# A gated mix of a state-space convolution and a bilinear GLU: the first TensorE work cut to a quarter of the zero columns, and new slack and ranks in the planner's tables

## The chip, the cores and the metric

The kernel runs on one NeuronCore of a Trainium2 chip. The metric is the device time of one execution in microseconds (us). Of each kernel there are timed runs, without a profile, and one profiled execution, whose trace tells what each engine did. The engines are TensorE (PE, with its weight loads shown apart as PEld), VectorE (DVE), ScalarE (ACT), GpSimd (POOL) and SyncE (SP). DMA transfers are issued here by SP and POOL, a few by ACT.

## The reference

For 2048 positions and 512 channels in float32 the reference mixes two results with a gate of one number per position:

```python
g = sigmoid((x * gate_w).sum(-1, keepdims=True))
a = A_ref(x, ...)      # y = irfft(rfft(u, 4096) * rfft(K, 4096))[:2048] + u * D_skip
b = B_ref(x, ...)      # ((x @ w_gate) * (x @ w_up)) @ w_down, inner width 1792
return g * a + (1 - g) * b
```

In A_ref, K[d, l] = 2 Re sum_n C[d, n] exp(A[d, n] dt[d] l) is a convolution kernel of 2048 taps per channel, from 128 complex states.

## The kernel before

**The GLU.** The inner width 1792 is 14 blocks of 128, in four groups of 3, 3, 4 and 4; the positions are four chunks of 512. For each group and chunk, `hidden` multiplies the tokens `xs` with the gate weights into the PSUM tile `pg` and with the up weights into `pu`; ACT copies `pg` to `h`, DVE multiplies by `pu`. `down` multiplies the product with the down weights into the PSUM tile `y` (two buffers), and `evacuate` has ACT scale it by 1 - g into `acc`. Every operand is split in two parts that the fast matmul format holds (`whi` and `wlo`, `dhi` and `dlo`, `hh` and `hl`), so that a product is three matmuls of 128x512, each with its own weight load. These are 2016 of the program's matmuls. The results of the groups are added up in DRAM by accumulating DMAs from POOL (`out<-acc`).

**The convolution.** It is a 4096-point transform done as small matmuls, all into PSUM tiles named `k` (four buffers): `k<-in,w2s` in the first part of the program transforms u (stored to DRAM as `su_d`); DVE and ACT build tables `x` and `v` for 32 channels at a time, and `k_block` makes the taps from them (`k<-v,x`, 64 matmuls); `k<-kt,w1k_t` is the first step of their transform (stored as `sk_d`). Then, for each quarter of the channels, four times: POOL loads a piece of `su_d` and of `sk_d` into `in` (two buffers), `m_second` transforms it (`k<-in,w2s`, in the last quarter `k<-x,w2s` and `k<-v,w2s`), `m_product` multiplies on DVE, and after every second piece `m_inverse` (`k<-y,w3s`) goes back and SP stores to `y_d`. `m_last` (`k<-in,w_t`, at the very end `k<-x,w_t`) makes the positions. These matmuls are float32, which the chip runs as two passes: two weight loads and two matmuls in the trace for one in the program.

**What sets the order.** Each piece of work is registered by `add` with its engine, an estimated duration, what it reads and writes, and a rank. `Work.plan` (L355) then places the pieces one by one: of those that are ready it takes the one with the earliest start, then the lowest rank, then the lowest number; the instructions are issued to the engines in that order, and each engine's queue runs strictly in it. Four tables of numbers bear on the change:

- `ready` (L279): a piece that reads what a transfer brings may be placed only `SURE` us behind the landing that the planner expects.
- `fetched` (L328): PE's program is brought in blocks of 256 instructions; `FETCH` (5.0 us) and `BEHIND` times the transfers then waiting say how late a block may be. PE's work is not placed ahead of that.
- `EASE` (L227): for a kind of work, named by engine, tiles and duration, an addition to its slack, rank or number.
- `count` and the duration of a piece feed both.

All recorded operations stand under line 124 in the profile, the helper that keeps each engine's order; so they are told apart by the tiles' names.

**The beginning.** `first_loads` (L577) clears a tile `acc` on DVE and has PE multiply it by itself into a scratch bank, before the first real data is there: two float32 matmuls of 512 columns.

Of the kernel before, what the change touches and what calls it, by code (L numbers as in the profile page):

```python
# [18 lines left out]
P = 128  # L19
# [150 lines left out]
class Bus:  # L170
# [25 lines left out]
    def add(self, task, at, us):  # L196
        at = max(at, self.now)
        self.serve(self.queues, self.now, at)
        self.now = at
        self.queues[task.engine == "pool"].append([task, us])  # L200
        self.loads.append((at, sum(x[1] for q in self.queues for x in q)))
        return self.serve([[[*x] for x in q] for q in self.queues], at, 1e9)


class Work:
# [16 lines left out]
    TABLE = 1.3  # L222
    ROOM = {"dve": 0.6, "act": 0.4}
    BEYOND = 60
    BEHIND = 1.05

    EASE = {  # L227
        "act:k/e:0.4": (3, 0, 0),
        "act:k/in:0.32": (0.0, 1, 0),
        "act:pb/x:0.31": (0.0, 0, -60),  # L230
        "act:raw/whi:0.62": (0.0, 0, -60),
        "act:t/rt:0.77": (0.0, 0, -200),
        "dve:ev/y:0.6": (3, 0, 0),
        "dve:k/kt:0.42": (0.0, -1, 0),
        "dve:m/v:1.09": (0.0, 0, -20),
        "pool:ts:0.95": (2, 0, 0),
        "sp:in:0.42": (0.0, 1, 0),
        "sp:ri:0.42": (2, 0, 0),
        "sp:w3s/w2s/v:1.3": (0.0, 1, 0),
    }  # L240
    DMA_RATE = 0.33

    SENT = {"sp": 1.15, "act": 1.15, "pool": 1.98}
    LANDED = {"sp": 1.79, "act": 1.79, "pool": 1.5}
    SURE = 2

    def __init__(self):
        self.tags, self.tasks = {}, []
# [30 lines left out]
    def ready(self, task, d):  # L279

        if d.engine == task.engine == "pe":
            return d.end
        if d.dma and d.start > 20.0 and task.engine in ("pe", "act", "dve"):
            return d.end + self.SURE
        return d.end + self.LAG.get(task.engine, 0.03) + (self.PE_LAG if d.engine == "pe" else 0.0)

    def inputs(self, task):
# [40 lines left out]
    def fetched(self, task, start, past, bus):  # L328
# [8 lines left out]
        while b < n1 + (self.BEYOND if step < 0.05 else 0):  # L337
            asked = self.passed(past, b - self.BLOCK - self.LEAD, n0, start, step)
            at = step * (b - n0) if b <= n1 else task.us + 0.11 * (b - n1)
            if asked < start:  # L340
                late = self.FETCH + self.BEHIND * min(bus.load(asked + 1.2), 5.0)
                start = max(start, asked + late - at)
# [107 lines left out]
def gated_mix_kernel(  # L450
# [16 lines left out]
    pe, dve, act, sp, pool_q = (InOrder(tc, e) for e in (nc.tensor, nc.vector, nc.scalar, nc.sync, nc.gpsimd))  # L467
# [3 lines left out]
    add = work.add  # L471
# [18 lines left out]
    def new(pool, tag, shape, dtype=F32, bufs=1, loose=False):  # L490
        return work.tile(pools[pool], tag, shape, dtype, bufs, loose)

    def bank():
        return new("ps_k", "k", [P, D], bufs=4, loose=True)
# [71 lines left out]
    def load_two(key, tile_of, src, one=True):  # L566

        t = tile_of([P, 2, D])
        for k in range(2):
            raws[key(k)] = (t, k)  # L570
        if one:
            add("sp", 0.42, lambda: sp.dma_start(t.t, src), w=[t], dma=512, rank=-1)
        return t

    ws, wd, xs = {}, {}, {}

    def first_loads():  # L577
        in_y = lambda shape: new("mid", "y", shape, bufs=2)
        in_ev = lambda shape: new("mid", "ev", shape, bufs=2)
        in_in = lambda shape: new("mid", "in", shape, bufs=2)  # L580
        xsrc = lambda kt: xT[P * kt : P * kt + P, :D]
        w0 = raws["w0"] = in_ev([P, 2, D])
        xt = [load_two(lambda k, n=n: ("x", 0, 0, 2 * n + k), in_y, None, False) for n in range(2)]
        wsrc = wts[0][:, : 2 * D].rearrange("p (k d) -> p k d", k=2)
        for kt in range(KT):

            t, k, ks = xt[kt // 2], kt % 2, slice(P * kt, P * kt + P)
            add("sp", 0.42, lambda t=t, k=k, kt=kt: sp.dma_start(t.t[:, k], xsrc(kt)), w=[(t, k)], dma=256, rank=-1)
            e, q = ("sp", sp) if kt else ("act", act)
            add(e, 0.42, lambda q=q, ks=ks: q.dma_start(w0.t[:, :, ks], wsrc[:, :, ks]), w=[(w0, ("k", kt))], dma=128, rank=-1)  # L590
        for f in (1, 2):
            load_two(lambda k, f=f: ("w", f, k), in_ev if f == 1 else in_in, wts[f][:, : 2 * D].rearrange("p (k d) -> p k d", k=2))


        zero = new("glu", "acc", [P, D], bufs=3)
        scratch = bank()
        add("dve", 0.2, lambda: dve.memset(zero.t, 0.0), w=[zero], rank=-1)

        def warm():
            for _ in range(2):  # L600
                pe.matmul(scratch.t, zero.t[:, :P], zero.t, start=True, stop=True)

        add("pe", 3.4, warm, r=[zero], w=[scratch], rank=-1, count=8)

    def weights(fs):
        for f in fs:
# [513 lines left out]
    def v_table(b):  # L1120
        ri, (su, di) = ris[b], sus[b]
        v = vtab["v"]

        def copies():
            for c in range(2):
                act.copy(v.t[:, c, :, 0:4], ri.t[:, c, :, W_B])
                act.copy(v.t[:, c, :, 36::4], ri.t[:, c, :, W_A])

        add("act", 1.46, copies, r=[ri], w=[(v, 2)])
        outer(  # L1130
            v, lambda: ri.t[:, :, :, W_A], lambda: su.t[:, :, W_A], lambda: ri.t[:, :, :, W_B],
            lambda: su.t[:, :, W_B], lambda: di.t[:, :, 0:4], [ri, su, di],
        )

        for to, of, n in (((33, 64, 2), (0, 16, 1), 16), ((34, 64, 4), (33, 49, 2), 8)):
            sq = new("tab", "sq", [P, TB, 16])
            dst = [lambda c=c, to=to: v.t[:, c, :, slice(*to)] for c in range(2)]
            src = [lambda c=c, of=of: v.t[:, c, :, slice(*of)] for c in range(2)]
            pair = lambda sq=sq, n=n: sq.t[:, :, :n]

            def sq_act(dst=dst, src=src, pair=pair):
                act.activation(dst[0](), src[0](), AF.Square)
                act.activation(pair(), src[1](), AF.Square)

            k = 0 if n == 16 else 1
            src_parts = [(v, ("r", 0)), (v, ("i", 0))] if k else [(v, 0), (v, 1), (v, 2)]
            us = 0.69 if n == 16 else 0.63
            add("act", 1.17 if n == 16 else 0.89, sq_act, r=src_parts, w=[(v, ("r", k)), sq])
            add(
                "dve", us,  # L1150
                lambda dst=dst, src=src: dve.scalar_tensor_tensor(
                    dst[1](), src[0](), 2.0, src[1](), op0=ALU.mult, op1=ALU.mult
                ),
                r=src_parts, w=[(v, ("i", k))],
            )
            tt(us, dst[0], dst[0], pair, ALU.subtract, [sq], [(v, ("r", k))])
        return v
# [331 lines left out]


    first_loads()
    prologue()
    for t in range(NR // 4):
# [8 lines left out]
    for b in range(NB):  # L1502
# [4 lines left out]
        v, old = v_table(b), x  # L1507
# [63 lines left out]
```

## Time and profile before

| | |
|---|---|
| timed runs | 584.66, 584.83, 585.61 us; median 584.83 us |
| profiled execution | 589.44 us, of which the span from first to last instruction is 587.5 us |
| PE busy | 576.0 us (98% of the span), 5996 matmuls and as many weight loads |
| DVE, ACT, POOL busy | 511.7, 399.1, 113.3 us (87%, 68%, 19%) |
| DMA | 136.28 MB, mean 232 GB/s |
| mean granted TensorE clock | 0.994 |

PE bounds the kernel: it is the work on 91% of the chain that ended last. A row of the timeline has the start in us, the duration in us (of merged rows from the first start to the last end, or the sum), engine, line, operation, tiles out<-in, and in brackets the time the engine stood idle before and what ended that. "issue" is idle time for which the profile shows no wait. A row of the windows view has the stretch, its length, each engine's busy time with the number of instructions, the granted clock, the DMA engines' share and GB/s. Since matmuls are pipelined and their ends modelled, a group of matmuls is best timed from start to start. Only a few idle spells of PE are in this trace, and the prediction shows them.

### The profile page before, as it was taken

The page shows a single profiled execution, that of the slowest core. Times are in us where ns is not written, and L with a number is a line of the kernel's source. Part 1 is how long each engine was busy: PE and PEld are TensorE (multiplying, and loading weights), DVE is VectorE, ACT ScalarE, POOL GpSimd, SP SyncE. Part 2 cuts the span into 40 slices and gives each one's busy share as a digit, 9 for nine tenths or more (in the row PEclk, how much of TensorE's full clock was granted, in tenths as well). Part 3 has the DMA queues.
Part 4 walks back from the last instruction along what each step waited for, and adds up shares of the span by engine and source line. Part 5 has one row for each costly group of instructions (what it writes and reads, how often), then busy time and mean ns, then how long its engine had stood idle before and what let it go on. Part 6 is the DMA issues. An engine that isn't in the chain of part 4 may idle for free.

```text
span 587.5 us, 14848 instructions
## 1 busy us (share of the span) xinstructions
PE 576.0 (98%) x5996; PEld 435.4 (74%) x5996; DVE 511.7 (87%) x812; ACT 399.1 (68%) x891; POOL 113.3 (19%) x159
## 2 busy tenths in 40 slices
PE   8999999989999999999999999999999999999995
PEld 5777777877887777888767678877778777777774
DVE  5999999977999999999999899996899998346745
ACT  4459978987568779975987585699858553333351
POOL 0003222410201141311122301133221004012011
PEclk9999999998999999999999999999999999999998
DMA  8999959996845798999879958889968259799686
GB/s 282 386 331 351 396 211 362 261 253 161 201 147 88 252 266 190 199 260 285 188 229 241 213 136 299 201 212 195 260 162 246 38 150 280 267 331 239 197 188 125
DMA packets 71687, 136.28 MB, mean 232 GB/s; under 512 B 6852, under 2 KB 35780, under 8 KB 69188
## 3 DMA queue, kind: packets, MB, share of 16 engines
q1 hardware_dynamic: 47668, 87.10, 43.0%
q0 software_dynamic: 23392, 47.98, 39.3%
q8 instruction: 47, 0.77, 0.5%
q10 hardware_dynamic: 560, 0.26, 0.2%
q14 instruction: 20, 0.16, 0.1%
HBM read 80.27 MB, written 55.05 MB: 230 GB/s over the span
## 4 chain that ended last, share of the span: by engine, by line
PE 91%; issue 4%; DMA 2%; POOL 1%; ACT 1%; DVE 1%; DVEq 0%; POOLq 0%; ACTq 0%
PE pg L124 26%; PE pu L124 26%; PE y L124 24%; PE k L124 15%; DMA in<-sk_d 1%; DMA y<-in_xT 1%; DMA sk_d<-ev 1%; POOL out L124 1%; POOL in L124 0%; ACT ev L124 0%; DVE y L124 0%; ACT h L124 0%; ACT xs L124 0%; DVE hl L124 0%; DVE dlo L124 0%
## 5 line engine op out<-in xcount | busy, mean ns | idle before, releaser
L124 PE MATMUL pu<-xs,whi 128*128 128x512 f32 x448 | 140.3, 395 | 0.0
L124 PE MATMUL pg<-xs,whi 128*128 128x512 f32 x448 | 139.4, 392 | 0.5 <-ACT whi L124 0.5
L124 PEld LDWEIGHTS pg<-xs,whi 128*128 128x128 f32 x448 | 84.7, 189 | 19.3 <-ACT whi L124 2.1
L124 PEld LDWEIGHTS pu<-xs,whi 128*128 128x128 f32 x448 | 85.4, 191 | 17.4
L124 PE MATMUL pg<-xs,wlo 128*128 128x512 f32 x224 | 90.6, 405 | 0.1
L124 PE MATMUL y<-dhi,hl 128*128 128x512 f32 x224 | 89.6, 400 | 0.6 <-DVE hl L124 0.6
L124 PE MATMUL pu<-xs,wlo 128*128 128x512 f32 x224 | 90.2, 403 | 0.0
L124 PE MATMUL y<-dlo,hh 128*128 128x512 f32 x224 | 87.4, 390 | 0.0
L124 PE MATMUL y<-dhi,hh 128*128 128x512 f32 x224 | 87.2, 389 | 0.0
L124 POOL DMA_DIRECT2D out<-acc x44 | 38.6, 955 | 167.9 <-ACT acc L124 160.0
L124 ACT COPY ev<-k 128x512 f32<-128x512 f32 x112 | 59.3, 598 | 16.5 <-PE k L124 16.5
L124 ACT CAST hh<-h 128x512 fp32r<-128x512 f32 x56 | 34.8, 622 | 45.8 <-DVE h L124 45.6
L124 DVE TENSOR_TENSOR h<-pu,h 128x512 f32<-128x512 f32 x56 | 38.6, 689 | 30.2 <-PE pu L124 29.7
L124 PEld LDWEIGHTS pu<-xs,wlo 128*128 128x128 f32 x224 | 42.6, 190 | 20.1 <-issue 11.4
L124 ACT ACTIVATE acc<-y,ngate 128x512 f32<-128x512 f32 x62 | 41.7, 685 | 22.7 <-PE y L124 20.5
L124 PEld LDWEIGHTS pg<-xs,wlo 128*128 128x128 f32 x224 | 42.4, 189 | 19.8 <-issue 9.5
L124 ACT COPY h<-pg 128x512 f32<-128x512 f32 x56 | 32.8, 586 | 34.9 <-PE pg L124 33.1
L124 PEld LDWEIGHTS y<-dhi,hl 128*128 128x128 f32 x224 | 42.0, 188 | 19.3 <-issue 7.7
L124 PEld LDWEIGHTS y<-dhi,hh 128*128 128x128 f32 x224 | 42.1, 188 | 9.0
L124 PEld LDWEIGHTS y<-dlo,hh 128*128 128x128 f32 x224 | 42.1, 188 | 7.8
L124 DVE TENSOR_TENSOR hl<-h,hh 128x512 fp32r<-128x512 f32 x56 | 38.4, 685 | 3.2 <-ACT hh L124 3.1
L124 PEld LDWEIGHTS k<-v,x 128*32 128x32 f32 x2048 | 29.4, 110 | 7.6 <-issue 7.2
(130 smaller groups left out, 962.9 us busy)
## 6 DMA issues: line engine op xcount, KB each, us to landing
xs<-xs_d SPq DMA_DIRECT2D x36, 512.0 KB, 6.7
out<-acc POOLq DMA_DIRECT2D x44, 256.0 KB, 6.1
raw<-in_wts SPq DMA_DIRECT2D x33, 256.0 KB, 4.5
xs_d<-xs SPq DMA_DIRECT2D x16, 512.0 KB, 7.6
su_d<-ev POOLq DMA_DIRECT2D x32, 256.0 KB, 7.2
y_d<-ts SPq DMA_DIRECT2D x28, 256.0 KB, 5.8
in<-su_d POOLq DMA_DIRECT2D x12, 512.0 KB, 6.6
sk_d<-ev SPq DMA_DIRECT2D x6, 1024.0 KB, 4.9
```

The lines of the kernel that those rows point to most:

```text
L124: got = getattr(self.engine, name)(*args, **kw)
```

## The change

Two kinds of edit. First, the clearing at the beginning covers 128 of the 512 columns, and PE's first work reads that quarter, repeated by a stride of zero: two matmuls of 512 columns as before and one of 128 behind them. Second, numbers of the planner: `BEHIND` goes from 1.05 to 1.3; `SURE` from 2 us for PE, ACT and DVE alike to 3 for PE and 2 for the others; and of the table `EASE`, five entries are dropped and five are new. The work in the program is otherwise the same; the order is planned anew.

```diff
-    BEHIND = 1.05
+    BEHIND = 1.3
     EASE = {
...
-        "act:k/in:0.32": (0.0, 1, 0),
+        "act:ts/xs:0.62": (0.0, 2, 0),
...
-    SURE = 2
+    SURE = {"pe": 3, "act": 2, "dve": 2}
...
-        if d.dma and d.start > 20.0 and task.engine in ("pe", "act", "dve"):
-            return d.end + self.SURE
+        if d.dma and d.start > 20.0 and task.engine in self.SURE:
+            return d.end + self.SURE[task.engine]
...
-        add("dve", 0.2, lambda: dve.memset(zero.t, 0.0), w=[zero], rank=-1)
+        add("dve", 0.06, lambda: dve.memset(zero.t[:, :P], 0.0), w=[zero], rank=-1)
 
         def warm():
-            for _ in range(2):
-                pe.matmul(scratch.t, zero.t[:, :P], zero.t, start=True, stop=True)
-
-        add("pe", 3.4, warm, r=[zero], w=[scratch], rank=-1, count=8)
+            w = zero.t[:, :P]
+            for n in (4, 4, 1):
+                to = scratch.t[:, : n * P].rearrange("p (n d) -> p n d", d=P)
+                rhs = w.unsqueeze(1).broadcast_to([P, n, P])
+                pe.matmul(to, w, rhs, start=True, stop=True)
+
+        add("pe", 3.85, warm, r=[zero], w=[scratch], rank=-1, count=12)
```

How the change moves instructions on PE is shown at four places. The first is the start of PE's program, as a piece of the difference (`acc` is the cleared tile, `k` the scratch bank):

```order
-L1565 UNCONDITIONAL_BRANCH
+L1568 UNCONDITIONAL_BRANCH
 L124 MATMUL k<-acc 128x512 x2
+L124 MATMUL k<-acc 128x128
 L124 MATMUL pg<-xs,whi 128x512 x2
 L124 MATMUL pg<-xs,wlo 128x512
```

One matmul of 128 columns, four PE instructions, stands between the old first work and the first real product.

The second place is the second block of taps, `k<-v,x`, with what stands ahead of it on PE; before:

```order
L124 MATMUL pg<-xs,whi 128x512 x2
L124 MATMUL pg<-xs,wlo 128x512
L124 MATMUL pg<-xs,whi 128x512 x2
L124 MATMUL k<-v,x 32x64 x64
L124 MATMUL pu<-xs,wlo 128x512
L124 MATMUL pu<-xs,whi 128x512 x2
```

and in the changed kernel:

```order
L124 MATMUL y<-dhi,hl 128x512
L124 MATMUL y<-dlo,hh 128x512
L124 MATMUL y<-dhi,hh 128x512
L124 MATMUL pg<-xs,wlo 128x512
L124 MATMUL pg<-xs,whi 128x512 x2
L124 MATMUL k<-v,x 32x64 x64
L124 MATMUL pg<-xs,wlo 128x512
L124 MATMUL pg<-xs,whi 128x512 x2
```

The block moves to an earlier place: counted from the start of PE's program (a matmul as two instructions, a float32 one as four) it begins with instruction 1480 before and with 1424 now.

The third place is in the second quarter of the channels, the third of its four `k<-in,w2s`. Before it stands 52 matmuls of 128x512 behind the second one, in the middle of GLU products:

```order
L124 MATMUL pg<-xs,wlo 128x512
L124 MATMUL pg<-xs,whi 128x512 x2
L124 MATMUL k<-in,w2s 32x512 x16
L124 MATMUL pu<-xs,wlo 128x512
L124 MATMUL pu<-xs,whi 128x512 x2
```

In the changed kernel 103 such matmuls, a `k<-v,x` block and a `k<-y,w3s` block lie between the second and the third:

```order
L124 MATMUL k<-y,w3s 64x128 x64
L124 MATMUL pg<-xs,wlo 128x512
L124 MATMUL pg<-xs,whi 128x512 x2
L124 MATMUL pu<-xs,wlo 128x512
L124 MATMUL pu<-xs,whi 128x512 x2
L124 MATMUL pu<-xs,wlo 128x512
L124 MATMUL pu<-xs,whi 128x512 x2
L124 MATMUL pu<-xs,wlo 128x512
L124 MATMUL pu<-xs,whi 128x512 x2
L124 MATMUL pu<-xs,wlo 128x512
L124 MATMUL pu<-xs,whi 128x512 x2
L124 MATMUL k<-in,w2s 32x512 x16
```

The loads for it keep their places on POOL: two `out<-ts`, then `in<-su_d`, `in<-sk_d`, the same pair again, then `out<-acc`.

The fourth place is PE's end. Before, the second half of `k<-x,w_t` stands directly ahead of the last two `y` tiles (24 matmuls):

```order
L124 MATMUL y<-dhi,hl 128x512
L124 MATMUL y<-dlo,hh 128x512
L124 MATMUL y<-dhi,hh 128x512
L124 MATMUL k<-x,w_t 32x512 x8
L124 MATMUL y<-dhi,hl 128x512
L124 MATMUL y<-dlo,hh 128x512
L124 MATMUL y<-dhi,hh 128x512
```

Now both halves stand together, 21 `y` matmuls ahead of those 24:

```order
L124 MATMUL y<-dhi,hl 128x512
L124 MATMUL y<-dlo,hh 128x512
L124 MATMUL y<-dhi,hh 128x512
L124 MATMUL k<-x,w_t 32x512 x16
L124 MATMUL y<-dhi,hl 128x512
L124 MATMUL y<-dlo,hh 128x512
L124 MATMUL y<-dhi,hh 128x512
```

Between the matmul that ends the last `y` tile but three and the first matmul of the last `y` tile but one, which needs its buffer, there were three `y` matmuls and half of `k<-x,w_t`; now there are the three `y` matmuls alone.

More of the change, by code (lines that the diff above doesn't have):

```diff
@@ L232 @@
         "act:t/rt:0.77": (0.0, 0, -200),
+        "act:ts/xs:0.62": (0.0, 2, 0),
         "dve:ev/y:0.6": (3, 0, 0),
-        "dve:k/kt:0.42": (0.0, -1, 0),
-        "dve:m/v:1.09": (0.0, 0, -20),
+        "dve:in/whi/wlo:0.69": (0.0, 1, 0),
+        "dve:k/in:0.42": (3, 0, 0),
+        "dve:k/ri:0.7": (0.0, 1, 0),
+        "pe:kt/k/ri/e:2.13": (0.0, 0, -200),
         "pool:ts:0.95": (2, 0, 0),
-        "sp:in:0.42": (0.0, 1, 0),
-        "sp:ri:0.42": (2, 0, 0),
         "sp:w3s/w2s/v:1.3": (0.0, 1, 0),
```

## Prediction

> **What bounds the kernel now.** I read the page first, then the list of waits of PE, then the timeline at each of those waits.
>
> ```profile
> PE 576.0 (98%) x5996; PEld 435.4 (74%) x5996; DVE 511.7 (87%) x812; ACT 399.1 (68%) x891; POOL 113.3 (19%) x159
> q8 instruction: 47, 0.77, 0.5%
> PE 91%; issue 4%; DMA 2%; POOL 1%; ACT 1%; DVE 1%; DVEq 0%; POOLq 0%; ACTq 0%
> ```
>
> PE is busy 98% of the span and is 91% of the chain that ended last. Its matmuls are the same in both kernels but for one small one, so an order can only win what PE idles or runs slowly. All its waits, in total, times and longest:
>
> ```profile
> PE k L124 <- issue: 1.8, 1, 1.8
> PE k L124 <- DVE acc L124: 1.5, 1, 1.5
> PE k L124 <- DMA in<-sk_d: 1.2, 1, 1.2
> PE y L124 <- DVE hl L124: 0.6, 1, 0.6
> PE pg L124 <- ACT whi L124: 0.5, 1, 0.5
> ```
>
> That is 5.6 us, of which 2.0 (1.5 and 0.5) are the beginning. The largest lies in the second block of taps; the rows are the timeline of PE, two stretches of the windows view, and the instruction queue in the DMA view from 129.8 to 130.8 us:
>
> ```profile
> 128.62 1.98 PE L124 MATMUL k<-v,x 128*32 128x64 f32 x125
> 132.36 0.30 PE L124 MATMUL k<-v,x 128*32 128x64 f32 x3 [1.76 <-issue]
> ...
> 130.20:133.65 3.45, 1.69 (x36) 1.25 (x26) 2.70 (x5) 1.84 (x11) 0.55 (x1) 1.00 0.76 150
> 133.65:137.06 3.41, 3.41 (x10) 2.63 (x9) 1.36 (x3) 2.61 (x7) 0.00 (x0) 0.50 0.47 141
> ...
> q8 instruction: 1, 0.02, 5.6%
> ```
>
> 125 of the block's 128 matmuls ran, then PE stood 1.76 us for nothing that waits on a semaphore. The page has 47 packets of 0.77 MB on the instruction queue, 16.4 KB each; 5996 matmuls and 5996 loads over 47 are 255 instructions a packet; and the one packet near lands in this second. So I read the stall as PE's own program coming late. In the stretch of 3.45 us around it PE worked 1.69, and in the next 3.41 the granted clock was 0.50, which costs half, 1.71 us.
>
> The second wait is for a transfer; the last row is the chain of waits:
>
> ```profile
> 317.82 1.60 POOL L124 DMA_DIRECT2D in<-su_d  x1
> 326.36 0.92 POOL L124 DMA_DIRECT2D in<-sk_d  x1 [6.94 <-issue]
> ...
> 331.52 1.15 PE L124 MATMUL k<-in,w2s 32*32 32x512 f32 x32 [1.16 <-DMA in<-sk_d]
> ...
> 326.36 4.91 DMA in<-sk_d
> ```
>
> POOL stood 6.94 us ahead of this load, it was under way 4.91 us, and PE waited the last 1.16.
>
> **The profiled time and the median.** The profiled execution took 589.44 us (span 587.5 and 1.94 around it). Less 1.76, 1.71 and 1.16 that is 584.81, and the timed median is 584.83. The agreement is closer than I may claim, but it says that the timed runs hold little of these three: their transfers are less crowded, or the parts differ and cancel. This decides the forecast, since what isn't lost in a timed run can't be won there.
>
> **The change, part by part.** *The beginning.* Rows of the timeline, then of the windows view:
>
> ```profile
> 0.92 0.48 DVE L124 MEMSET acc<- 128x512 f32 x1 [0.92 <-PEq L1560]
> 1.39 0.17 DVE L124 MEMSET skip<- 128x128 f32 x1
> 1.46 3.78 PE L124 MATMUL k<-acc 128*128 128x512 f32 x4 [1.46 <-DVE acc L124]
> 5.30 0.40 ACT L124 CAST whi<-ev 128x256 fp32r<-128x256 f32 x1
> 5.75 1.22 PE L124 MATMUL pg<-xs,whi 128*128 128x512 f32 x2 [0.51 <-ACT whi L124]
> 9.76 1.05 PE L124 MATMUL pu<-xs,whi 128*128 128x512 f32 x2
> 11.62 0.62 PE L124 MATMUL pu<-xs,whi 128*128 128x512 f32 x2
> ...
> 3.95:7.36 3.41, 2.90 (x6) 1.34 (x5) 1.88 (x4) 2.12 (x5) 0.00 (x0) 1.00 1.10 354
> 7.36:10.77 3.41, 3.41 (x10) 2.64 (x9) 3.24 (x15) 2.18 (x6) 0.00 (x0) 1.00 0.97 335
> ```
>
> A quarter of the columns is cleared in about 0.17 us (the row of `skip`, the same shape) in place of 0.48: PE starts 0.31 us sooner, at 1.15. The added matmul is two passes of a quarter of 3.78/4, 0.47 us. The first work ends at 1.15 + 3.78 + 0.47 = 5.40, where it ended at 5.24. The first real product still waits for ACT's `whi`, which ends at 5.70: on the path this is 0, and PE idles 0.35 us there in place of 0.51.
>
> What it could move is the clock. Two matmuls took 1.05 us at 9.76 and 0.62 at 11.62, so PE ran at half speed until about 10.77, although the clock column says 1.00 there. Laying the 3.41 us of the slow stretch back from 10.77: the stretch to 10.77 was wholly busy and full speed followed; the one to 7.36 was busy 2.90 of 3.41 (85%) and did not bring it. With 0.16 us less idle that is 3.06, 90%. Nothing says that 90% does what 85% didn't, so I take 0.
>
> The Trainium skill ("TensorE: Matmul & The Clock Gate", "What's actually happening") says that the full clock is granted after a busy window of about 3.4 us, and that the windows run free of the kernel's start. The trace agrees with the length (3.41). By that rule the gain depends on how the windows fall in each run, and it is the second rival.
>
> If the clock did rise at the first work, the gain is bounded by DVE, which feeds PE here:
>
> ```profile
> 13.93 0.69 DVE L124 TENSOR_TENSOR h<-pu,h 128x512 f32<-128x512 f32 x1 [1.59 <-PE pu L124]
> 25.15 0.69 DVE L124 TENSOR_TENSOR h<-pu,h 128x512 f32<-128x512 f32 x1 [0.28 <-PE pu L124]
> ```
>
> DVE waited for PE 1.59 and 0.28 us up to the place at 28 us where PE waits for DVE (0.6, `hl`): a faster PE wins at most 1.87 us and then waits longer there.
>
> *The second block of taps* (`BEHIND`). A block of PE's program ends at the same instruction number in both orders. The stall came after 249 or so of the block's 256 instructions, number 1480 + 249 = 1729. In the new order the block has 1424 to 1679, and 1729 falls behind it, among GLU matmuls. What counts is PE's time over the instructions between the asking for a packet and its need. A stretch of the same number of instructions that reaches back over the block holds 249 short and the rest long ones before, 256 short ones now: seven long ones fewer. Long ones take 113 ns, from the row
>
> ```profile
> 16.88 2.72 PE pu L124 x12
> ```
>
> (12 matmuls and 12 loads, 2.72/24). So PE comes there 0.79 us sooner, and `BEHIND`, meant to hold such work back, does not lengthen the lead here. With the profiled transfers the stall would be 1.76 + 0.79 = 2.55. In a timed run without a stall before it is 0 to 0.79; I take 0, since the lighter transfers that hid it leave unknown room. Below nothing is excluded.
>
> The Trainium skill ("Runtime: NRT & Kernel Launch", "Instruction fetch mechanics") holds that fetching is hidden, as dispatch is slower than the refill. By it this place costs 0 in every run and the slower rival falls away. The trace disagrees with 1.76 us in a block that issues 250 instructions in 1.98.
>
> *The third `k<-in,w2s`* (`SURE` 3 for PE). Between the second and third there are 51 more GLU matmuls (51 x 0.227 = 11.6 us) and two `k` blocks of about 2 us each: 15 us more cover, while POOL's order there stays. The wait of 1.16 is gone. What is late next: the fourth piece stands right behind, but its loads follow the third's directly on POOL, so the cover holds for it too. In a timed run that is between 0 and -1.16; by the agreement above I take 0.
>
> *The end.* Rows of the timeline:
>
> ```profile
> 573.75 0.40 PE L124 MATMUL y<-dhi,hh 128*128 128x512 f32 x1
> 574.19 1.37 ACT L124 ACTIVATE acc<-y,ngate 128x512 f32<-128x512 f32 x2 [1.62 <-PE y L124]
> 574.76 1.09 PE L124 MATMUL k<-x,w_t 64*32 64x512 f32 x16
> 575.78 0.50 PE L124 MATMUL y<-dhi,hl 128*128 128x512 f32 x1
> 581.14 0.39 PE L124 MATMUL y<-dhi,hh 128*128 128x512 f32 x1
> 581.57 0.88 DVE L124 SCALAR_TENSOR_TENSOR kt<-y,ngate,kt 128x256 f32<-128x256 f32 x2 [0.28 <-PE y L124]
> ```
>
> The matmul at 573.75 ends a `y` tile; ACT starts on it 0.44 us later and one of its two takes 0.69, so the buffer is free at 574.88. Three `y` matmuls behind leave PE ready at 573.75 + 4 x 0.227 = 574.66; before, half of `k<-x,w_t` (1.02 us to 575.78) covered the rest. Now nothing does: +0.22. One run of `k` less saves one change between shapes; no row shows it alone, 0 to 0.2 from the 0.1 by which `k` rows overlap what follows; -0.1. From 581.14 to the end the same DVE steps and stores follow.
>
> *The other entries of* `EASE` reorder work that lies beside PE. Queue for queue I found no consumer of a transfer on PE that stands clearly closer to its load, so 0; DVE, 87% busy, is their cover, and a table that came late would cost its lateness on PE.
>
> Sum for the timed median: 584.83 + 0 + 0 + 0 + 0.22 - 0.1 = **584.9 us**, no change.
>
> **Rivals.** 0.2%, 1.17 us, is about what a measurement of this kernel can tell from no change.
>
> 1. *The timed runs do hold the transfer wait*, and the agreement was chance. Then 584.83 - 1.16 + 0.12 = 583.8. For: the load is late by POOL's 6.94 us, not by a hair. Against: the sum. Still within 0.2%; only with a little more it is faster.
> 2. *The clock rises during the first work.* Then up to 1.87 is won: 583.1. For: the busy spell at the beginning grows from 3.78 to 4.25 us, 0.84 longer than one stretch instead of 0.37, so if the stretches fall anywhere, in 25% instead of 11% of runs one lies wholly inside. Against: in the other runs nothing moves, and a median of few runs shows mostly those.
> 3. *Slower: PE's program comes late behind the second block* at instruction 1729. The stall is up to 2.55 us, and from the point where it empties about half of a stretch, as 1.69 of 3.45 did, the clock halves for 3.41 us, 1.71 more: up to 584.83 + 2.55 + 1.71 + 0.12 = 589.2; with half the stall and the slow clock 587.9, with the stall alone 586.2 to 587.5. For: the lead is shorter. Against: the timed runs showed nothing of it before.
> 4. *The planner's numbers don't act*: the waits of PE come out as before. Then 584.9 again.
>
> **How the numbers follow.** The forecast with rival 4 0.40, rival 1 0.20, rival 2 0.15, rival 3 0.18, and 0.07 for a new wait elsewhere of a microsecond or two. Faster: 0.15, 0.08 of rival 1 and 0.05 from the edge of the forecast, 0.28. Slower: 0.18 and the 0.07, 0.25. Same: the rest, 0.47. The range runs from rival 2 (583.1, and a little) to rival 3 without the full price: 583.0 to 587.4. The forecast's own range is 583.8 to 585.7.
>
> **What would show it.** In the new profile: PE's first work at about 1.15 and the first product still at 5.75; the clock up near 10.8; no wait of PE for `in<-sk_d` around 330; an "issue" wait or none behind the second `k<-v,x`; a wait of about 0.2 us of `y` for ACT ahead of the last two tiles; from the last matmul to the end 6 us. The forecast is wrong if PE's waits sum to over a microsecond more or less than what the timed runs held, or if the time moves without them.

## The result, and the profile after

The changed kernel is faster. Over 22 runs of each, side by side, it takes 581.98 us (581.00 to 584.79) against 585.56 us (581.94 to 589.93) before: a ratio of 0.9935, with a 95% interval of 0.9917 to 0.9952. The forecast of 584.9 us and its range from 583.0 are missed by 2.9 and 1.0 us. The profiled execution after took 581.93 us, with a span of 580.1.

The page after, its rows of busy time and of the chain's shares by engine:

```profile
PE 573.5 (99%) x5998; PEld 433.8 (75%) x5998; DVE 510.9 (88%) x812; ACT 401.6 (69%) x891; POOL 113.5 (20%) x159
...
PE 97%; DMA 1%; ACT 1%; DVE 1%; issue 0%; DVEq 0%; ACTq 0%
```

The list of PE's waits after (us in total, times, longest):

```profile
PE k L124 <- DVE acc L124: 1.1, 1, 1.1
PE pg L124 <- ACT h L124: 0.7, 1, 0.7
PE y L124 <- DVE hl L124: 0.6, 1, 0.6
PE pg L124 <- ACT whi L124: 0.4, 1, 0.4
```

The waits for "issue" (1.8) and for `in<-sk_d` (1.2) are gone; a new one for ACT's `h` (0.7) has come. The timeline after, at the beginning, the second taps, the third `k<-in,w2s` of the second quarter, the new wait, and the end:

```profile
1.06 4.21 PE L124 MATMUL k<-acc 128*128 128x512 f32 x6 [1.06 <-DVE acc L124]
5.62 1.17 PE L124 MATMUL pg<-xs,whi 128*128 128x512 f32 x2 [0.35 <-ACT whi L124]
6.86 0.62 PE L124 MATMUL pu<-xs,whi 128*128 128x512 f32 x2
...
121.05 1.99 PE L124 MATMUL k<-v,x 128*32 128x64 f32 x128
...
343.43 1.14 PE L124 MATMUL k<-in,w2s 32*32 32x512 f32 x32
...
421.71 0.50 PE L124 MATMUL pg<-xs,wlo 128*128 128x512 f32 x1 [0.67 <-ACT h L124]
...
575.99 0.39 PE L124 MATMUL y<-dhi,hh 128*128 128x512 f32 x1
576.41 0.88 DVE L124 SCALAR_TENSOR_TENSOR kt<-y,ngate,kt 128x256 f32<-128x256 f32 x2 [1.97 <-PE y L124]
577.32 0.36 ACTq L124 DMA_DIRECT2D out<-kt  x1
```

Two matmuls take 0.62 us from 6.86 on, so full speed began at 6.6, where it began at 10.8 before. All 128 matmuls of the taps run through in 1.99 us. The row at 343.43 has no wait. And one thing stands at the end that no part of the prediction has: from PE's last product to the end of the span it is 580.1 - 575.99 = 4.1 us, where it was 587.5 - 581.14 = 6.4 us. So there are four candidates for 3.6 us: the beginning (theory C in the expectations below), PE's late program with the slow clock behind it (theory P), the transfer (theory T), and the end (theory E).

### The profile page after: what moved, and what is told of

The parts are those of the page before. It is cut to its first block, busy times and chain, and to the rows that moved or that the text cites. A ratio compares the mean times of both kernels' runs of the same rounds, so it can differ in the third digit from the quotient of the medians.

```text
span 580.1 us, 14843 instructions
## 1 busy us (share of the span) xinstructions
PE 573.5 (99%) x5998; PEld 433.8 (75%) x5998; DVE 510.9 (88%) x812; ACT 401.6 (69%) x891; POOL 113.5 (20%) x159
## 4 chain that ended last, share of the span: by engine, by line
PE 97%; DMA 1%; ACT 1%; DVE 1%; issue 0%; DVEq 0%; ACTq 0%
PE pg L124 27%; PE y L124 27%; PE pu L124 27%; PE k L124 16%; DMA y<-in_xT 1%; ACT h L124 0%; DVE y L124 0%; ACT acc L124 0%; ACT xs L124 0%; DVE hl L124 0%; DVE dlo L124 0%; DVE kt L124 0%; DVEq L1568 0%; ACT whi L124 0%; DVE h L124 0%
## 5 line engine op out<-in xcount | busy, mean ns | idle before, releaser
L124 PE MATMUL pu<-xs,whi 128*128 128x512 f32 x448 | 138.2, 390 | 0.0
L124 PEld LDWEIGHTS pu<-xs,whi 128*128 128x128 f32 x448 | 84.1, 188 | 17.0
L124 PEld LDWEIGHTS pg<-xs,wlo 128*128 128x128 f32 x224 | 42.1, 188 | 21.5 <-issue 10.1
L124 DVE TENSOR_TENSOR v<-m,v 128x896 f32<-128x896 f32 x32 | 34.0, 1084 | 0.2
```

Of the source, the lines that this page charges most:

```text
L124: got = getattr(self.engine, name)(*args, **kw)
```

## The experiments

Of the kernel before there were between 17 and 30 runs beside each of the four sets of experiments, with medians of 585.60, 585.18, 586.26 and 585.34 us. "Order of before" means that every engine's instructions stand row by row as in the kernel before, but for the edit.

**1. The changed order with the old first work.**

```diff
-        add("dve", 0.06, lambda: dve.memset(zero.t[:, :P], 0.0), w=[zero], rank=-1)
+        add("dve", 0.06, lambda: dve.memset(zero.t, 0.0), w=[zero], rank=-1)
...
-            for n in (4, 4, 1):
...
+            for _ in range(2):
+                pe.matmul(scratch.t, zero.t[:, :P], zero.t, start=True, stop=True)
```

> The changed kernel in its own order, with only PE's first work as it was before (128x512 cleared, two matmuls of 512 columns). The order of everything else is the changed kernel's, row by row; PE's program is 4 instructions shorter at the front. Theory P (the timed runs of the kernel before do hold PE's late program behind the second taps, 1.76 us, and the slow clock after it, 1.71, and the new order loses them): the first work is worth little, 582.0 to 582.5 us, where the changed kernel has 581.98; in the profile full speed is reached near 10.8 us. Theory C (the gain is the clock that rises sooner at the beginning): most of the gain goes, 583.5 to 585.0. Theory T (the gain is the transfer in<-sk_d and the rest of the order): as P, 582.0 to 582.5.

Measured: 582.23 us (7 runs, 581.59 to 583.16), 0.25 more than the changed kernel, which is within the spread of the runs. The beginning isn't where most of the gain comes from. And the clock rose early with the old work too. The windows view of this kernel, with the stretch that ends where full speed began:

```profile
3.11:6.52 3.41, 2.95 (x5) 0.98 (x4) 1.08 (x3) 1.62 (x4) 0.00 (x0) 1.00 1.02 323
```

**2. The order of before with the new first work; 3. with 24 more instructions ahead of it; 4. with both.** Run 2 has the first work of the change. Run 3 keeps the full clearing and cuts the two matmuls of 512 columns into eight of 128, so that each of PE's program packets begins 24 instructions earlier in the work. Run 4 has nine matmuls of 128 columns on the cleared quarter, 28 instructions.

```diff
-            for _ in range(2):
-                pe.matmul(scratch.t, zero.t[:, :P], zero.t, start=True, stop=True)
+            for _ in range(2):
+                for n in range(4):
+                    pe.matmul(scratch.t[:, n * P : n * P + P], zero.t[:, :P], zero.t[:, n * P : n * P + P], start=True, stop=True)
```

That is run 3; run 4, where `w` is the cleared quarter, has this in place of the two:

```diff
+            for n in range(9):
+                pe.matmul(scratch.t[:, n % 4 * P : n % 4 * P + P], w, w, start=True, stop=True)
```

> The kernel before in its own order, with only PE's first work as in the change (a quarter cleared, two matmuls of 512 columns and one of 128, all reading the quarter); the planner's numbers for it are left, so the order is the one before, row by row, and PE's program is 4 instructions longer at the front. Theory P: within 0.5 us of the kernel before (585.56 over 22 runs), so 585.0 to 586.0; the stall behind the second taps may be there or not in its profile. Theory C: 583.3 to 584.3, as DVE's waits allow at most 1.87 us, and full speed from 6.6 us in the profile. Theory T: 585.0 to 586.0.

> The kernel before in its own order and with its own full clearing; only the two first matmuls of 512 columns are cut into eight of 128 over the same columns. This adds 24 instructions at the front of PE's program (32 in place of 8) and so moves every boundary of its packets 24 instructions earlier in the work. At the second taps the asking then falls 24 long instructions sooner (24 x 0.113 = 2.7 us) and the need 24 short ones sooner (0.2 us): 2.5 us more lead than the 11.77 of the profile before. Theory P: the stall of 1.76 and the slow clock of 1.71 go: 585.56 less 1.8 to 3.5 is 582.1 to 583.8, and the runs lie closer together than the 8 us of the kernel before. Theories C and T: 585.2 to 586.0, with the spread unchanged.

> The kernel before in its own order with both: a quarter cleared as in the change, and the first work cut into nine matmuls of 128 columns that read it (36 instructions in place of 8, so the packets' boundaries lie 28 instructions earlier; the first work's columns are those of the change). Nothing of the planner's new order is in it. Theory P alone: 582.1 to 583.8. Theory C alone: 583.3 to 584.3. P and C together: 580.2 to 582.5, so as fast as the change without its order. Theory T: 585.2 to 586.0.

Measured, with 585.60 before: 583.24 us (582.52 to 584.38), 583.51 (582.56 to 584.79) and 582.99 (582.57 to 584.31), 12 runs each. Moving the packets without touching the columns is worth 2.1 us, in timed runs, as theory P has it. But run 2 gave as much, against P's expectation and near theory C's 583.3 to 584.3, and the two do not add up in run 4. Run 2 has 4 more instructions ahead of the work as well, so it could be the boundary there too; and in run 3's profile full speed began at 7.14 us, not near 10.8, so the beginning could have a share there.

**5. Only 4 instructions, without the new first work.** The second matmul of 512 columns is cut into two of 256.

```diff
-            for _ in range(2):
-                pe.matmul(scratch.t, zero.t[:, :P], zero.t, start=True, stop=True)
+            pe.matmul(scratch.t, zero.t[:, :P], zero.t, start=True, stop=True)
+            for n in range(2):
+                pe.matmul(scratch.t[:, 2 * n * P : 2 * n * P + 2 * P], zero.t[:, :P], zero.t[:, 2 * n * P : 2 * n * P + 2 * P], start=True, stop=True)
```

> The kernel before in its own order, with its full clearing; only the second of PE's two first matmuls is cut into two of 256 columns. The columns are the same, PE's program is 4 instructions longer at the front, as with the change's first work, and the first work starts and ends as before. It separates what the run with the change's first work left mixed (583.24 us, against 585.6 before). Theory P (the packet's boundary at the second taps, moved by 4 instructions, gives 0.45 us more lead, and that is enough): 583.0 to 584.2. Theory C' (it is the earlier start and the clearing, not the boundary): 585.2 to 586.0. If the clock at the beginning were late in part of the runs whatever the first work is, both kernels would hold it and the difference here would still be only the boundary's.

Measured: 583.47 us (582.51 to 585.42, 12 runs), against 585.18 before; ratio 0.997 (0.9952 to 0.9989). PE's second taps in its profile:

```profile
128.58 1.99 PE L124 MATMUL k<-v,x 128*32 128x64 f32 x128
```

The stall is gone. Four instructions at the front, with the same work in the same time, are worth 1.7 us (0.6 to 2.8 by the interval), and full speed began late here too, at 10.66 us. With the new first work it is 0.23 less (run 2), which the spread of the runs does not resolve. Theory P holds for the timed runs.

**6. The kernel before, unchanged, profiled once more.**

> The kernel before, unchanged, for a second profile of it. Theory P (the late program at the second k<-v,x belongs to this order, not to one execution): a wait of 1 to 2 us named issue at the second k<-v,x again, with the packet landing 9 to 11 us after the asking. If the profile before caught a rare run: no such wait.

This execution took 586.39 us. Two rows of the list of PE's waits:

```profile
PE k L124 <- issue: 1.9, 1, 1.9
PE k L124 <- DMA in<-sk_d: 1.4, 1, 1.4
```

And PE's timeline at the second taps:

```profile
126.98 1.98 PE L124 MATMUL k<-v,x 128*32 128x64 f32 x125
130.85 0.30 PE L124 MATMUL k<-v,x 128*32 128x64 f32 x3 [1.89 <-issue]
```

Both waits are there again, at the same places. Full speed began at 7.6 us this time, and no slow clock followed the stall. So the stall isn't the mark of one execution. And it is PE's program: counted over all of PE's records, the stall stands ahead of number 1730 in both profiles, and the stalls of over a microsecond in experiments 7 and 10 stand ahead of 1730, 4802 and 6594, which lie whole multiples of 256 apart.

**7. What the packet waits for.** The packet is seen to land in the DMA view. When PE asks for it isn't in the trace; I take the start of PE's instruction 320 ahead of the packet's first one (matmuls and weight loads counted); this is an assumption. For run 5 and for the second profile of before, the DMA view of the microsecond in which it landed:

```profile
q8 instruction: 1, 0.02, 5.9%
```

(run 5, 123.9 to 124.9 us), and the same for before (128.5 to 129.5 us):

```profile
q8 instruction: 1, 0.02, 5.6%
```

| order of before | asked | landed | after us | stall of PE |
|---|---|---|---|---|
| before, first profile | 120.59 | 130.74 | 10.1 | 1.76 |
| before, second profile | 118.96 | 129.49 | 10.5 | 1.89 |
| run 5 (4 earlier) | 120.10 | 124.88 | 4.8 | none |
| run 2 (4 earlier) | 117.92 | 122.38 | 4.5 | none |
| run 3 (24 earlier) | 115.98 | 122.27 | 6.3 | none |

The first row and run 5 have the late clock at the beginning, which puts both some 2 us later. Four instructions sooner are 0.45 us at the 113 ns of a long one, and the packet lands over 5 us sooner. It is the same in all profiles of this order: without the move it took 9.8 to 10.5 us (four profiles: the two of the table, that of the next edit, and that of `BEHIND` alone in experiment 10, whose order is the old one there), with a move of 4 to 28 instructions 4.5 to 6.9 (seven). A constant time to land would not do that. My guess was that the packet is asked for on the other side of something in the queues, and SP's `raw`, issued 1.14 us ahead of the asking in the kernel before, was the suspect.

```diff
-        for t in self.plan():
+        order = self.plan()
+        raw, late = (next(t for t in order if t.engine == "sp" and t.n == n) for n in (513, 499))
+        order.remove(raw)
+        order.insert(order.index(late) + 1, raw)
+        for t in order:
             t.fn()
```

> The kernel before with PE's program, its packets' boundaries and PE's order untouched; on SP's queue the raw load that stands between two and one out stores (at 119.45 us in the profile before) goes out behind the one store instead, some 3 us later, at about 122.8. Theory Q (what decides is on which side of this transfer the packet is asked for): in the profiles of this same order of SP the packet asked for 1.14 and 1.15 us after that raw was issued took 10.14 and 9.82 us to land, and the one asked 0.69, 0.11 or less after it took 4.8, 4.5 and 6.3. Then the packet is now ahead of it and lands some 5 us after the asking, the stall is gone at an unchanged boundary, and the time is as with the boundary moved by 4, 583.0 to 584.0, where the kernel before has 585.2 to 585.6. Theory L (PE's lead alone decides, the transfers don't matter): the stall stays, 585.0 to 586.0. If the later raw makes ACT's cast late (its slack is about 1 to 2 us): a wait of PE a few us behind, and 584 to 586 with the packet early all the same.

Measured: 586.42 us (582.57 to 589.22, 12 runs), against 586.26. SP's timeline in this run, where the moved `raw` goes out with the next one:

```profile
120.74 1.00 SPq L124 DMA_DIRECT2D raw<-in_wts  x2
```

And PE's timeline at the second taps:

```profile
130.13 0.30 PE L124 MATMUL k<-v,x 128*32 128x64 f32 x3 [1.65 <-issue]
```

The `raw` went out 3 us later and the packet still took 10.2 us. Theory Q falls. Whether the packet queued behind something else stays open: that it lands 5 us sooner when four instructions more stand at the front is measured, the reason isn't.

**8. The transfer on another queue.** Run 3, with the third piece's `in<-sk_d` on SP, which stood idle there.

```diff
-                lambda w=w, rows_m=rows_m: pool_q.dma_start(
+                lambda w=w, rows_m=rows_m: (sp if w and (q, T) == (1, 2) else pool_q).dma_start(
```

> The kernel with the packets 24 instructions earlier (583.51 us), with one more thing: the transfer in<-sk_d for the third k<-in,w2s of the second quarter goes out on SP's queue in place of POOL's. In its profile POOL stood 7.11 us ahead of it, while SP stood idle from 313.34 to 326.98. PE waited for this transfer 1.16 us in the profile before, and 0.29, 0.43 and 1.6 in the three since in that order. Theory T (this wait is held in timed runs, and is the rest of the gain that the packets' boundary and the first work don't account for, 583.0 to 582.0): the wait is gone and the time is 582.3 to 583.0. If the rest of the gain is elsewhere in the order: 583.2 to 583.8, with the wait gone all the same. If SP issues it late or it holds up what stands behind it on SP (w2s, pb): slower than 583.5.

Measured: 582.79 us (581.88 to 584.76, 12 runs), 0.72 less than run 3 (582.56 to 584.79). The two overlap widely, and the kernel before was itself 0.42 us lower beside this run, so the pair alone doesn't show a gain. SP's row for the transfer, in the timeline:

```profile
310.03 0.38 SPq L124 DMA_DIRECT2D in<-sk_d  x1
```

And PE's row for the third piece:

```profile
324.34 1.14 PE L124 MATMUL k<-in,w2s 32*32 32x512 f32 x32
```

No wait is left. In the seven profiles with this load on POOL in the order of before the wait was 1.2, 0.4, 0.3, 1.6, 0.3, 0.9 and 1.4 us, 0.9 in the mean, so a gain of that size in timed runs would fit theory T; the next run decides it.

**9. The three together in the order of before** (run 4 with the edit of run 8).

> The order of the kernel before with three edits together: PE's first work as in the change (a quarter cleared), cut into nine matmuls of 128 columns so that the packets lie 28 instructions earlier, and the transfer in<-sk_d for the third k<-in,w2s on SP's queue. Without the last it had 582.99, and the last was worth 0.7 us (583.51 to 582.79). If the causes add up: 582.1 to 582.5, and what is left to the changed kernel's 581.98 is the rest of its order, 0.1 to 0.5 us. If the rest of the order is worth nothing: 581.7 to 582.1. If the first work brings nothing: 582.6 to 583.0.

Measured: 582.02 us (6 runs, 581.89 to 582.71). Three small edits, without any of the planner's new numbers, give the changed kernel's time. Against run 4, which lacks only the transfer's edit, it is 0.97 us less, and the two hardly overlap (run 4 from 582.57 on): theory T holds, with 0.7 to 1.0 us by the two pairs. Against run 8 the new first work is worth 0.77 here.

**10. One part of the planner's numbers alone.** `BEHIND` at 1.3 in the kernel before; and `SURE` by engine in the kernel before.

```diff
-    BEHIND = 1.05
+    BEHIND = 1.3
```

> The kernel before with only BEHIND at 1.3 and the order that the planner then makes. PE's order is the one before, row by row, up to row 656 of 1640, so the second taps, their packet and the lead there are those of before. Theory P: the gain at the second taps is not there; 584.5 to 586.5, by what the order behind row 656 happens to bring, and the profile may show the stall of 1 to 2 us at the second k<-v,x. If BEHIND is what brings the gain: 582.0 to 583.5.

> The kernel before with only the slack behind landings by engine (3 us for PE in place of 2; nothing else differs) and the order that the planner then makes. Its second taps begin at instruction 1423 of PE, as in the change (1424 there with 4 more at the front), so the block lies wholly ahead of the boundary at which the kernel before stalled. Theory P: the stall is gone with this part alone, 582.0 to 584.0. Theory T: the third k<-in,w2s has its cover as in the change, which belongs to the same figure. If the gain is of several parts that only together bring it: 584.5 to 586.

Measured: 595.41 us (592.93 to 598.29) and 597.79 us (595.74 to 599.72), 6 runs each: ratios of 1.0179 and 1.0216. Each part alone is slower by 10 to 13 us, which no theory expected. With `BEHIND`, the largest row of PE's waits:

```profile
PE k L124 <- issue: 3.1, 4, 1.2
```

and two rows of PE's timeline, at the second taps and at the very end:

```profile
129.73 0.30 PE L124 MATMUL k<-v,x 128*32 128x64 f32 x3 [1.21 <-issue]
...
577.47 1.09 PE L124 MATMUL k<-x,w_t 64*32 64x512 f32 x16 [0.47 <-issue]
```

With `SURE`, the largest row of PE's waits:

```profile
PE k L124 <- issue: 4.3, 3, 2.1
```

the row of PE's timeline with the longest of these three:

```profile
263.11 0.69 PE L124 MATMUL k<-y,w3s 32*64 32x128 f32 x3 [2.09 <-issue]
```

and the stretch in the windows view behind it, with the granted clock at 0.50:

```profile
263.08:266.50 3.42, 3.39 (x10) 2.48 (x11) 1.01 (x2) 0.87 (x2) 0.00 (x0) 0.50 0.92 226
```

With `BEHIND` alone PE's order is the old one up to row 656, and the stall at the second taps is there as in the kernel before: theory P again. The rest is new. The program comes late at other places, once with the slow clock behind it. The last of these waits in each, 0.47 and 0.56 us ahead of the second `k<-x,w_t`, are of another kind: they don't stand at a packet's first instruction. And most of the loss is at the end. The planner put the last `k<-x,w_t` behind all `y`, so that ACT, DVE and the stores follow it: with `BEHIND` it is 592.6 - 577.97 = 14.6 us from PE's last matmul to the end, with `SURE` 597.9 - 583.44 = 14.4, where it was 6.4. An order is found for the numbers as a whole; the worth of one number can't be read by setting it alone.

**11. A longer first work in the changed kernel.** The last small matmul has 224 columns in place of 128.

```diff
-            for n in (4, 4, 1):
+            for n, d in ((4, P), (4, P), (2, 112)):
```

> The changed kernel with the last small matmul of PE's first work at 224 columns in place of 128 (96 more, 0.35 us more), the same number of instructions and the same order. PE then works from 1.06 to about 5.6 without the 0.35 us of idle time ahead of the first product, so every stretch of 3.41 us behind the first is wholly busy. In ten profiles so far a stretch with 2.88 to 2.95 us of work brought the clock twice and failed three times, one with 3.06 or more never failed. Theory K (3.06 of 3.41 is already always enough): 581.7 to 582.3, as the changed kernel (581.98), with full speed at 4.5 to 8 us. Theory K' (the idle 0.35 us still costs a late clock in some runs, which are those above 583.4, 5 of 22): the median 581.5 to 581.9 and no run above 583.4. If the first product is held up by the longer first work: up to 0.1 slower.

Measured: 582.16 us (581.52 to 582.59, 6 runs). The changed first work is long enough; six runs are too few to say more of the upper end.

**12. The end.** Run 9 and the changed kernel have the same time, yet PE's last product starts at 573.97 us in the profile of the one and at 575.99 in that of the other. The same 56 pieces of work are the last in both orders. One run puts those of run 9 into the changed kernel's order, the other those of the changed kernel into the old order; `end` is the list of their numbers.

```diff
-        for t in self.plan():
+        order = self.plan()
+        last = {t.n: t for t in order[-len(end):]}
+        for t in order[: -len(end)] + [last[n] for n in end]:
             t.fn()
```

> The order of the kernel before with the three edits (582.02 us), and with the last 56 pieces of work put into the order that the changed kernel has there (the same 56 pieces on both sides; the two halves of k<-x,w_t then run as one, ahead of y, and the last two out<-x go out from POOL some 3 and 8 us earlier before PE's last product). Theory E (the changed kernel's end is worth about 1.9 us by itself: from PE's last product to the end of the span 4.1 us there against 6.1 with the old end; on PE it costs 0.26 for the y tile that waits for ACT and saves about 0.5 for one run of k less): 579.9 to 580.5, faster than both kernels. Theory F (the end is set by the last store in any order, and the shorter end of the changed kernel only mirrors something ahead of it): 581.7 to 582.3, with 6 us behind the last product again.

> The changed kernel with its last 56 pieces of work put into the order that the kernel before has there; nothing else is changed. Theory E: from PE's last product to the end 6.0 us in place of 4.1, 1.9 us more, less the 0.26 of the y tile and plus about 0.5 for one more run of k: 583.6 to 584.4. Then the changed kernel's gain of 3.6 us holds this end too, and its order loses about 2 us to the order before elsewhere on PE (the wait of pg for h, 0.7, among it). Theory F: 581.7 to 582.3.

Measured: 580.59 us (6 runs, 580.14 to 581.52), ratio 0.9908 (0.9873 to 0.9942); and 583.85 us (12 runs, 583.17 to 584.75). The new end is worth 1.4 us on the old order and 1.9 on the new. Theory E holds from both sides, and the first of these kernels beats both the kernel before and the changed one. Rows of POOL, PE and ACT in its timeline:

```profile
566.87 2.89 POOL L124 DMA_DIRECT2D out<-x  x2 [6.97 <-DVE x L124]
...
574.08 0.39 PE L124 MATMUL y<-dhi,hh 128*128 128x512 f32 x1
...
575.41 0.35 ACTq L124 DMA_DIRECT2D out<-kt  x1
```

and SP's queue (`q1`) and POOL's (`q0`) in its DMA view, from ACT's store to the end (packets, MB, share of 16 engines):

```profile
q1 hardware_dynamic: 253, 0.32, 30.2%
...
q0 software_dynamic: 12, 0.00, 1.3%
```

The same rows in the timeline of the changed kernel with the old end:

```profile
573.03 1.28 POOL L124 DMA_DIRECT2D out<-x  x1 [1.43 <-DVE kt L124]
...
575.43 0.39 PE L124 MATMUL y<-dhi,hh 128*128 128x512 f32 x1
...
576.77 0.35 ACTq L124 DMA_DIRECT2D out<-kt  x1
```

and the two queues in its DMA view, from 576.7 us to the end:

```profile
q1 hardware_dynamic: 438, 0.67, 34.4%
q0 software_dynamic: 385, 0.19, 29.1%
```

With the old end, POOL's last accumulating store `out<-x` goes out 2.4 us before PE's last product and is still moving when the last store `out<-kt` goes out; from that store to the end it takes 582.03 - 576.77 = 5.3 us. With the new end POOL's queue is all but empty by then (12 packets) and it takes 578.3 - 575.41 = 2.9 us. SP's four stores `out<-kt` start earlier too, 4.4 us ahead of PE's last product in place of 1.6, and leave 0.32 MB for this stretch in place of 0.67. So that the new order of these pieces shortens the end is shown; how much of it is POOL's stores and how much SP's isn't, since no run moves the one without the other.

## Why the prediction was wrong, step by step

**The step that failed first: "it says that the timed runs hold little of these three".** The profiled time less three losses came to 584.81, next to a median of three runs of 584.83, and I took the agreement as a sign that timed runs don't pay the losses. Two things were wrong with it. Three runs say little about a kernel whose runs spread over 8 us: the median of 22 is 585.56. And the profiled execution held a fourth loss which I left in, the late clock at the beginning. Runs 2 and 5 differ in the first work alone; in their profiles full speed began at 5.03 and at 10.66 us, and PE's last product started at 574.49 and 576.67, with the same waits between, about 2.2 us apart:

```profile
574.49 0.39 PE L124 MATMUL y<-dhi,hh 128*128 128x512 f32 x1
...
576.67 0.39 PE L124 MATMUL y<-dhi,hh 128*128 128x512 f32 x1
```

Less that too, the profiled time is 584.81 - 2.2 = 582.6, and 582.79 is what the order of before takes with the stall and the transfer wait gone (run 8). So timed runs do hold them, some 2 us for the program (1.7 in run 5, 2.1 in run 3) and 0.7 to 1.0 for the transfer. By the second profile the same subtraction gives 586.39 - 1.89 - 1.40 = 583.1, and the median lies 2.5 us above that.

The slow clock behind the stall, the 1.71 of that subtraction, is in a part of the timed runs. Each run's record has its mean granted clock: it is 0.994 or 0.995 in 19 of the 87 runs of the kernel before beside the experiments, as in its first profile (0.994), and these have a median of 587.2 us against 585.2 for the others. In none of the 66 runs of experiments 2 to 5, 8 and 9, which have no stall there in their profiles, is it below 0.996. A stretch of 3.41 us at half clock takes 0.003 off the mean of such a run, so I read the 19 as runs with the slow clock; where it stood in them isn't recorded.

**The second taps.** That the block's new place shortens the lead was right: counted as in experiment 7, it is 9.4 us from asking to need (119.15 to 128.55) against 11.77 with the stall of 1.76, so 10.0 without it: 0.6 less, where 0.79 was said. That the stall would therefore be 0 to 0.79 us, or 2.55, was wrong, because the time to land isn't a constant: 5.3 us there after the change, 10.1 to 10.5 before. I also put the move down to `BEHIND`; with `BEHIND` alone the block keeps its place (run 10), and with `SURE` alone it moves. Rival 3 (slower) fell with it.

The Trainium skill ("Runtime: NRT & Kernel Launch", "Instruction fetch mechanics") has fetching hidden behind dispatch. By it run 5, four instructions and no other work, would have been worth nothing; it was worth 1.7 us, and the measurement decides.

**The third `k<-in,w2s`.** The cover was right and the wait is gone; taken as 0, it was worth 0.7 to 1.0 us. That is rival 1, whose 583.8 was too high only because the rest wasn't in it.

**The beginning.** PE starts at 1.06 (1.15 was said) and the first product at 5.62 (5.75 was said), so that start itself wins 0.13 us at most: right in the main. "Nothing says that 90% does what 85% didn't" was half right. Full speed came late in three of seven profiles with the old columns in two or three matmuls (at 10.77 us before, 10.66 in run 5, 10.50 with `SURE` alone) and in none of seven with the cleared quarter, wide, cut or lengthened (7.23 at the latest). A stretch with 2.82, 2.90 or 2.91 us of work in 3.41 didn't bring it, ones with 2.88 and 2.95 did, and those with 3.04 or more always did. The old first work stands on the edge, the new one beyond it. Since the old one fails in only part of the runs, the worth over runs is less than rival 2's 1.87: 0.2 to 0.8 us by the pairs (0.23 and 0.77 above, 0.25 in the changed order), of which 0.23 and 0.25 lie within the spread of the runs.

The rule of the Trainium skill ("TensorE: Matmul & The Clock Gate", "What's actually happening"), that the stretches run free of the kernel's start, agrees: with one and the same first work full speed came at 5.83, 6.41, 6.52, 7.60, 10.50, 10.77 us.

**The end.** "From 581.14 to the end the same DVE steps and stores follow", and "from the last matmul to the end 6 us": this is the other term that failed. I looked at PE's side of the move of `k<-x,w_t`, 0.22 for the `y` tile (measured: 0.26), and not at what depends on `k<-x,w_t`, which is the last stores of POOL and SP. POOL's `out<-x` took 6.6 us to land in the kernel before, where SP's `out<-kt` of the same size took 4.5, and the last store was moved in the same stretch as both. It landed 4.2 us after its issue with the old end and 1.9 with the new (the profiles of experiment 12). The new order there was worth 1.4 to 1.9 us. The run of `k` less, taken as -0.1, saves about 0.25, by the matmuls' starts around it in the two profiles.

**Other entries of** `EASE`, **taken as 0.** The new order loses about 1.8 us on the way: with the old end it takes 583.85, the old order with the three edits 582.02. The wait of `pg` for ACT's `h` is 0.6 to 0.7 of it; the rest is spread over small gaps and I haven't placed it.

So the 3.6 us are, from the runs: about 2 for PE's program, 0.7 to 1.0 for the transfer, 0.2 to 0.8 for the first work and 1.4 to 1.9 for the end, less about 1.8 that the new order gives back. These add up to about 2.5 to 3.9. The first three were priced by edits to the old order, where they come to 3.5 together (585.56 to 582.02); that the changed order wins the same for each is argued from its waits, not measured.

## What to carry to other kernels

A profiled execution less its waits is no measure of what timed runs hold: profile the kernel a second time, and look for losses that are no waits, such as a late clock, before taking a coincidence for a reason. When work is moved near the end, follow everything that depends on it down to the last store, on every queue. And where PE's program is long, a few instructions more at the front can move a stall away: it costs one run to try.

## What the runs showed of the hardware that was not expected

A packet of PE's program asked for four instructions sooner (0.45 us) landed over 5 us sooner (10.1 to 10.5 us after the asking against 4.5 to 4.8, with the asking counted as in experiment 7), and PE went on 1.35 to 1.62 us after a late packet had landed, in all six stalls of a microsecond or more. The slow clock followed the stall of 1.76 us in the first profile of before and one of 2.09 us with `SURE` alone, not the stalls of 1.89, 1.65, 1.64 and 1.21 us. A last store of 128 KB took 5.3 us to the end of the span where POOL's and SP's stores had 0.86 MB left to move beside it, and 2.9 us where they had 0.32 MB.
